# Two tiles of x begin 8 and 16 bytes behind a multiple of 256 bytes

## The chip, the cores and the metric

The kernel runs on one core of a Trainium2 chip. The metric is the device time of one execution in microseconds (us), as the median of several runs. The core has a matrix engine (TensorE, PE in the profile; its weight loads are listed apart as PEld), a vector engine (DVE), a scalar engine (ACT), a general engine (POOL) and an engine that only issues transfers (SP). Each works through its own queue in order.

## The reference

Attention over queries that are averaged in pairs, and a feed-forward block behind it:

```python
q_pool = q.reshape(B, H, S // 2, 2, D).mean(axis=3)      # B=8 H=8 S=1152 D=64
scores = scale * np.matmul(q_pool, k.transpose(0, 1, 3, 2))
attn = np.exp(scores - np.max(scores, axis=-1, keepdims=True))
attn = attn / (np.sum(attn, axis=-1, keepdims=True) + 1e-09)
x = np.matmul(attn, v)                   # then to 4608 tokens x 512
h = x @ w_in                             # 512 -> 2048
out = (h - np.tanh(h)) @ w_out           # 2048 -> 512
```

Everything is float32.

## The kernel before

**Attention.** Heads are handled in 32 pairs, one head on each half of the 128 partitions. Float32 precision is reached by splitting a value into a high part that TensorE takes in one pass (type F32R, tiles kq_h) and the rest (kq_l), and adding the products high x high, high x low and low x high. Each pair's 576 queries are done in two halves of 288 columns. The unnormalised result of a pair goes to a scratch tensor in memory, x_dram, and the sums of the exponentials to s_dram; their reciprocals come back through r_dram.

**Feed-forward.** The 4608 tokens are done in nine chunks of 512, and the 2048 inner columns in 16 steps of 128, so there are 144 steps. A step has two products. `hidden` makes 12 matmuls of 512 columns into ps_h: the stationary operand is a block of w_in (high or low), the moving operand a block x[:, c] of x_h or x_l, c = 0 to 3; eight of the twelve read x_h and four x_l. `shrink` computes h - tanh(h) on ACT, DVE and POOL, and splits it into g_hi and g_lo. `second` makes 12 matmuls of 512 columns into ps_o, with g as the stationary and w_out as the moving operand. Steps 0 to 2 are placed among the last three attention pairs; from about 796 us on only feed-forward steps are left. The last step of all does its `hidden` in two halves of 256 columns.

**x.** An object of class X holds one chunk's tiles. `fetch` brings 512 tokens of x_dram into the tile x_l in one transfer. `fetch_r` spreads the reciprocals over the partitions of x_r. For each c, `times` multiplies x_l by x_r into x_r, `high` copies that to x_h in the type F32R (ACT), and `low` writes the difference to x_l. For the first chunk these steps lie beside attention, with `times` and `low` on DVE; for the other eight they lie beside the steps of the chunk before, with `times` and `low` on POOL at steps 7 to 14, and the transfer issued at step 4 (for the second chunk, ahead of the loop). Chunks alternate between two pools of tiles, xp[0] and xp[1], each with one x_h and one x_l.

**Order.** The engines' queues are written by hand: the wrapper InOrder keeps the order of the program on each engine, which is why nearly all instructions carry its line, L37. The planner has no say in it. In front of the feed-forward the lengths of the tiles (x, the reciprocals, weights, g) are multiples of 256 bytes a partition, and they follow each other in memory in the order in which their pools are made; x of the first pool is the first of them.

**A start that is off, elsewhere.** The raw weights, 64 bits wide, are loaded twice from the same source: into w_raw at its start, and right behind it into w_off one 16-bit element in (`self.off[:, 1:4 * WN + 1]`).

Of the kernel before, what the change touches and what calls it, by code (L numbers as in the profile page):

```python
# [8 lines left out]
F32R = mybir.dt.float32r  # L9
# [37 lines left out]
def attention_ffn_kernel(  # L47
# [16 lines left out]
    P = 128  # L64
    B, NP, _, _, SQ = q.shape
# [26 lines left out]
    xp = [ctx.enter_context(tc.tile_pool(name="xp0", bufs=1))]  # L92
# [17 lines left out]
    class X:  # L110


        def __init__(self, ci):
            self.t0, self.n = chunks[ci]
            self.h = xp[ci % 2].tile([P, NP, 512], F32R, name="x_h")
            self.l = xp[ci % 2].tile([P, NP, 512], F32R, name="x_l")
            self.r = {}

        def fetch(self):
# [109 lines left out]
    with ExitStack() as actx:  # L229
# [27 lines left out]
        def psum():  # L257
            return ring.tile([P, 2, 512], F32, name="ps")
# [298 lines left out]
        for pi in range(n_pair):  # L557
# [7 lines left out]
            n = pi + EARLY - n_pair  # L565
            if n == 0:
                c = Chunk(0)
# [5 lines left out]
            for place in range(NS):  # L573
# [3 lines left out]
                if kt == 0:  # L577
                    o = psum()
# [28 lines left out]
    for ci in range(len(chunks)):  # L607
        if ci:
            c = Chunk(ci)
# [4 lines left out]
        for f in range(NF):  # L614
            n = ci * NF + f
# [76 lines left out]
```

## Time and profile before

| | us |
|---|---|
| median of 3 runs | 1580.07 |
| lowest and highest run | 1576.46 and 1581.28 |
| the profiled execution | 1580.02 |
| its span, from the first to the last instruction | 1578.3 |
| PE busy in the span | 1556.5 |
| DVE, POOL, ACT busy | 1185.8, 1155.3, 978.3 |

The granted clock of TensorE over the span was 0.999. In the profile's rows a group is named by line, engine, operation and tiles, written out<-in, with the shape as partitions x elements and a count; then come busy us, mean ns of one, and idle us ahead of it. In the timeline a row has start, length, and how many instructions were merged in it. Matmuls overlap in the records, so that their pace is read from their starts. DMA rows give packets, MB, and the share of 16 engines that the packets took.

### The profile page before, as it was taken

How to read it: one execution, taken by the hardware profiler on the slowest of the kernel's cores; microseconds unless marked ns; L12 is line 12 of the kernel's file. 1: busy time of each engine (PE TensorE's matmuls, PEld its weight loads, DVE VectorE, ACT ScalarE, POOL GpSimd, SP SyncE). 2: the span in 40 equal slices, each digit the busy share in tenths (PEclk: the TensorE clock that was granted, in tenths of full speed). 3: DMA queues.
4: the chain of work that ended last, by engine and by line, in shares of the span. 5: the costliest groups of instructions: out<-in, count | busy, mean ns of one | idle time of the engine just before them, and what ended most of it. 6: DMA issues, size and time to landing. Idle time of an engine off the chain costs nothing.

```text
span 1578.3 us, 30802 instructions
## 1 busy us (share of the span) xinstructions
PE 1556.5 (99%) x12012; PEld 1224.1 (78%) x12012; DVE 1185.8 (75%) x1558; ACT 978.3 (62%) x1617; POOL 1155.3 (73%) x813
## 2 busy tenths in 40 slices
PE   7999999999999999999999999999999999999998
PEld 5777777777777777676778888888888888888886
DVE  6588787888888887765457777777777777777776
ACT  5667667667667667675645655565555555565654
POOL 6788888898888897785857576666767575766664
PEclk9999999999999999999999999999999999999999
DMA  5757767768677769573171201010010101020000
GB/s 169 207 177 218 222 185 220 218 211 252 186 237 210 218 201 267 143 231 91 63 285 70 68 15 67 14 61 14 13 61 14 67 14 67 14 67 14 28 1 27
DMA packets 88676, 193.59 MB, mean 123 GB/s; under 512 B 12882, under 2 KB 39890, under 8 KB 86482
## 3 DMA queue, kind: packets, MB, share of 16 engines
q1 hardware_dynamic: 79746, 155.35, 27.4%
q0 software_dynamic: 8784, 36.28, 12.7%
q8 instruction: 94, 1.54, 0.4%
q14 instruction: 52, 0.43, 0.1%
HBM read 126.12 MB, written 38.04 MB: 104 GB/s over the span
## 4 chain that ended last, share of the span: by engine, by line
PE 91%; DMA 3%; ACT 2%; DVE 2%; issue 1%; SPq 0%; POOLq 0%; POOL 0%; ACTq 0%; DVEq 0%
PE ps L37 43%; PE ps_o L37 24%; PE ps_h L37 24%; ACT p L37 2%; DMA s_dram<-s_s 2%; DVE mx L37 1%; DMA m_row<-m_dram 0%; DMA x_r<-r_dram 0%; DMA m_dram<-tr 0%; DVE w_hl L37 0%; SPq L37 0%; DVE w_t L37 0%; DMA q<-in_q_dram 0%; DVE ps_w L37 0%; DVE x_r L37 0%
## 5 line engine op out<-in xcount | busy, mean ns | idle before, releaser
L37 DVE TENSOR_REDUCE mx<-ps 128x2 f32<-128x768 f32 x448 | 400.1, 924 | 145.2 <-PE ps L37 145.0
L37 POOL TENSOR_SCALAR g_m<-g_u 128x512 uint8<-128x512 f32 (+1 forms) x145 | 247.2, 1705 | 184.6 <-ACT g_u L37 170.3
L37 POOL TENSOR_TENSOR sum<-p,p 128x576 f32<-128x576 f32 x192 | 294.4, 1533 | 117.9 <-ACT p L37 117.9
L37 ACT ACTIVATE p<-ps 128x576 f32<-128x576 f32 x576 | 347.3, 653 | 48.0 <-PE ps L37 27.6
L37 POOL TENSOR_TENSOR sum<-sum,p 128x576 f32<-128x576 f32 x192 | 291.7, 1519 | 15.0
L37 PE MATMUL ps<-p,v 128*64 128x288 f32 x2304 | 286.4, 407 | 3.5 <-DVE mx L37 0.4
L37 PE MATMUL ps<-kq_h 64*128 64x288 f32 (+1 forms) x1920 | 273.4, 338 | 8.4 <-ACT kq_h L37 6.4
L37 PEld LDWEIGHTS ps<-p,v 128*64 128x64 f32 x2304 | 162.5, 137 | 119.6 <-ACT p L37 10.2
L37 POOL TENSOR_TENSOR g_lo<-g_s,g_hi 128x512 fp32r<-128x512 f32 (+1 forms) x145 | 186.9, 1289 | 87.4 <-ACT g_hi L37 87.4
L37 PE MATMUL ps_o<-w,g_hi 128*128 128x512 f32 x792 | 244.0, 389 | 1.0 <-ACT g_hi L37 1.0
L37 ACT ACTIVATE g_u<-ps_h 128x512 f32<-128x512 f32 (+1 forms) x142 | 84.0, 591 | 217.8 <-PE ps_h L37 216.3
L37 PEld LDWEIGHTS ps<-kq_h 64*128 64x128 f32 x1920 | 179.1, 186 | 49.6 <-issue 13.9
L37 DVE SCALAR_TENSOR_TENSOR ps_w<-g_u,ps_h 128x512 f32<-128x512 f32 (+1 forms) x142 | 98.4, 693 | 153.2 <-ACT g_t L37 153.2
L37 PE MATMUL ps_h<-x_h,w 128*128 128x512 f32 (+1 forms) x800 | 212.0, 387 | 0.1
L37 ACT ACTIVATE g_s<-g_u,pc 128x512 f32<-128x512 f32 x290 | 193.4, 715 | 11.4 <-POOL g_lo L37 0.2
L37 PE MATMUL ps<-m_row,sel 64*128 64x288 f32 x1152 | 171.4, 293 | 2.8 <-DMA m_row<-m_dram 2.2
L37 PEld LDWEIGHTS ps_o<-w,g_hi 128*128 128x128 f32 x792 | 148.5, 188 | 32.1 <-ACT g_hi L37 1.4
L37 PEld LDWEIGHTS ps_h<-x_h,w 128*128 128x128 f32 x800 | 149.3, 188 | 31.1 <-DVE g_t L37 0.5
L37 PE MATMUL ps<-kq_l,kq_h 64*128 64x288 f32 x1152 | 171.7, 293 | 0.0
L37 PE MATMUL ps<-kq_h,kq_l 64*128 64x288 f32 x1152 | 171.6, 293 | 0.0
L37 PE MATMUL ps_o<-w,g_lo 128*128 128x512 f32 x396 | 154.4, 390 | 0.1
L37 DVE COPY_PREDICATED g_s<-g_m,g_t 128x512 f32<-128x512 uint8 (+1 forms) x145 | 110.5, 762 | 17.0 <-POOL g_m L37 2.1
(114 smaller groups left out, 2379.7 us busy)
## 6 DMA issues: line engine op xcount, KB each, us to landing
kq_l<-raw POOLq DMA_DIRECT2D x31, 864.0 KB, 8.0
v<-in_v_dram SPq DMA_DIRECT2D x32, 576.0 KB
raw<-in_k_dram SPq DMA_DIRECT2D x31, 576.0 KB
x_dram<-o_s SPq DMA_DIRECT2D x32, 288.0 KB
x_l<-x_dram SPq DMA_DIRECT2D x9, 1024.0 KB
out_dram<-o_f SPq DMA_DIRECT2D x36, 256.0 KB
raw<-in_q_dram SPq DMA_DIRECT2D x30, 288.0 KB
raw<-in_q_dram POOLq DMA_DIRECT2D x30, 288.0 KB, 10.0
```

The costliest lines, as they stand in the source:

```text
L37: i = f(*args, **kwargs)
```

## The change

The tiles x_h and x_l are made 64 elements longer (2112 float32 values a partition instead of 2048). The data takes 2048 of them: in x_h from element 2 on (8 bytes), in x_l from element 4 on (16 bytes). All uses go through self.h and self.l, and so through the shifted view. No instruction is added, removed or moved.

```diff
         def __init__(self, ci):
             self.t0, self.n = chunks[ci]
-            self.h = xp[ci % 2].tile([P, NP, 512], F32R, name="x_h")
-            self.l = xp[ci % 2].tile([P, NP, 512], F32R, name="x_l")
+
+            self.h, self.l = (xp[ci % 2].tile([P, NP * 512 + 64], F32R, name=n)[:, o:o + NP * 512].rearrange(
+                "p (c n) -> p c n", c=NP) for n, o in (("x_h", 2), ("x_l", 4)))
             self.r = {}
```

## The prediction

> **What bounds the kernel now.** I read the page's busy shares first, then the stretches of the span, then the timeline of TensorE inside one stretch, and last the tiles that the change touches.
>
> ```profile
> span 1578.3 us, 30802 instructions
> PE 1556.5 (99%) x12012; PEld 1224.1 (78%) x12012; DVE 1185.8 (75%) x1558; ACT 978.3 (62%) x1617; POOL 1155.3 (73%) x813
> PE 91%; DMA 3%; ACT 2%; DVE 2%; issue 1%; SPq 0%; POOLq 0%; POOL 0%; ACTq 0%; DVEq 0%
> ```
>
> TensorE is busy 99% of the span and carries 91% of the chain that ended last. DVE, ACT and POOL stay at 75% or below. A busy PE could still hide waits, so the stretches (columns: length, then busy us and instructions of PE, weight loads, DVE, ACT, POOL, then clock):
>
> ```profile
> 100.00:900.00 800.00, 793.22 (x8110) 601.30 (x8108) 609.40 (x724) 522.76 (x839) 641.41 (x447) 1.00 0.65 193
> 1200.00:1300.00 100.00, 100.00 (x442) 82.78 (x442) 75.35 (x109) 59.51 (x103) 66.80 (x47) 1.00 0.09 32
> 796.20:1570.00 773.80, 406.67 (x1704) 318.29 (x1704) 194.54 (x283) 165.54 (x284) 1.00 0.14 48
> ```
>
> The third row counts only instructions on ps_h, the product of x with w_in. So 1704 of the matmuls that read x lie in the feed-forward stage, where TensorE is busy 100.00 of 100 us; the last stretch, after 796 us, is one unbroken stream of matmuls, at granted clock 1.00. Anything that x's address does to a matmul there goes straight into the time, and anything that it does to another engine is hidden until that engine runs out of slack.
>
> The timeline shows what one such matmul costs (start, length, and a group of so many):
>
> ```profile
> 1474.54 1.07 PE L37 MATMUL ps_h<-x_l,w 128*128 128x512 f32 x4
> 1475.44 1.07 PE L37 MATMUL ps_h<-x_h,w 128*128 128x512 f32 x4
> 1476.35 0.61 PE L37 MATMUL ps_o<-w,g_hi 128*128 128x512 f32 x2
> 1476.80 0.39 PE L37 MATMUL ps_o<-w,g_lo 128*128 128x512 f32 x1
> ...
> 1479.98 1.07 PE L37 MATMUL ps_h<-x_l,w_raw 128*128 128x512 f32 x4
> ...
> 1559.43 0.64 PE L37 MATMUL ps_h<-x_l,w 128*128 128x256 f32 x4
> 1559.91 1.12 PE L37 MATMUL ps_h<-x_h,w 128*128 128x256 f32 x8
> ```
>
> Starts, not lengths, give the price, since the lengths overlap. Four of 512 columns take 1475.44 - 1474.54 = 0.90 us, and the four behind them 0.91: 226 to 227 ns each. Four of 256 columns take 1559.91 - 1559.43 = 0.48 us, 120 ns each. So 256 columns cost about 106.6 ns (0.416 ns a column), and about 13.4 ns of each matmul do not depend on its columns. x_h, x_l and the second product (1476.80 - 1476.35 = 0.45 for two) all run at the same pace today.
>
> **The change, part by part.** It adds no instruction, no transfer and no wait, and moves none on any queue. x_h and x_l become 64 elements longer (2112 instead of 2048 a partition); the data starts 2 elements (8 bytes) in for x_h and 4 elements (16 bytes) in for x_l. Each tile is 256 bytes longer, so what lies behind in memory shifts by 512 bytes and keeps its place against 256. What can change is the time of the instructions that touch x:
>
> ```profile
> L37 PE MATMUL ps_h<-x_l,w x400: 283/389/389, 810.9 to 1561.2; 128*128 128x512 f32 x131, 128*128 128x256 f32 x3
> L37 POOL TENSOR_TENSOR x_r<-x_l,x_r x32: 1284/1294/1307, 828.1 to 1470.0; 128x512 f32<-128x512 f32 x32
> L37 POOL TENSOR_TENSOR x_l<-x_r,x_h x32: 1290/1299/1302, 834.3 to 1476.2; 128x512 fp32r<-128x512 f32 x32
> L37 SPq DMA_DIRECT2D x_l<-x_dram x9: 385/386/577, 598.3 to 1407.1; - x9
> L37 DVE TENSOR_TENSOR x_r<-x_l,x_r x4: 650/974/1887, 614.5 to 683.2; 128x512 f32<-128x512 f32 x4
> L37 DVE TENSOR_TENSOR x_l<-x_r,x_h x4: 627/904/1126, 618.3 to 684.5; 128x512 fp32r<-128x512 f32 x4
> L37 ACT ACTIVATE x_h<-x_r x36: 631/634/637, 615.8 to 1471.4; 128x512 fp32r<-128x512 f32 x36
> ```
>
> *The matmuls.* 1704 in the feed-forward stage and 36 (three steps of 12) before it make 1740; two thirds read x_h (1160), one third x_l (580). The trace has no matmul whose moving operand starts 8 or 16 bytes off. The nearest is the query half: both halves are 288 columns of one tile, the first at its start, the second 1152 bytes in, which is 128 behind a multiple of 256.
>
> ```profile
> 405.25 0.29 PE L37 MATMUL ps<-kq_h 64*128 64x288 f32 x2
> 405.38 0.29 PE L37 MATMUL ps<-kq_l,kq_h 64*128 64x288 f32 x2
> 405.51 0.30 PE L37 MATMUL ps<-kq_h,kq_l 64*128 64x288 f32 x2
> ...
> 410.36 0.29 PE L37 MATMUL ps<-kq_h 64*128 64x288 f32 x2
> 410.49 0.29 PE L37 MATMUL ps<-kq_l,kq_h 64*128 64x288 f32 x2
> 410.62 0.30 PE L37 MATMUL ps<-kq_h,kq_l 64*128 64x288 f32 x2
> ```
>
> The pairs follow each other by 0.13 us in the first half (405.25, 405.38, 405.51) and in the second (410.36, 410.49, 410.62). So 128 bytes off costs nothing, and I take 0. Bounds: from below, the 13.4 ns that do not depend on columns, gone altogether: -1740 x 13.4 = -23 us. From above, the slowest pace at which this program streams columns. The plain f32 product of p and v has, per pair of 288 columns,
>
> ```profile
> L37 PE MATMUL ps<-p,v 128*64 128x288 f32 x2304 | 286.4, 407 | 3.5 <-DVE mx L37 0.4
> ```
>
> 286.4 us over 1152 pairs, 249 ns or 0.865 ns a column against 0.416. At that pace a matmul of x costs 0.449 x 512 = 230 ns more: 1160 x 230 = +267 us for x_h alone, +400 for both.
>
> The Trainium skill, page "SBUF — State Buffer", section "Specifications (TRN2)", says that the memory is read in lines of 16 bytes, that two hits on a line are needed for full bandwidth, and that each step to a new line is paid for. By it x_l, 16 bytes off, keeps 128 lines a matmul, and x_h, 8 bytes off, touches 129, the two end lines with two hits each; if the extra line costs the time of four columns (an estimate: 4 x 0.416 = 1.7 ns), the sum would be 1160 x 1.7 = +1.9 us higher. No run here shows it, and it would be too small to tell from no change.
>
> *The transfer into x_l*, nine times 1 MB. A row for a start that is off exists: the raw weights are loaded twice from the same source, once into w_raw at its start and, issued directly behind it, into w_off 2 bytes in. Two windows, the first while the copy into w_raw runs, the second while the one into w_off does (queue: packets, MB, share of 16 engines):
>
> ```profile
> q1 hardware_dynamic: 253, 1.03, 71.6%
> q0 software_dynamic: 108, 0.21, 31.5%
> ...
> q1 hardware_dynamic: 570, 1.44, 101.4%
> ```
>
> 71.6% of 16 engines over 3.6 us is 41.2 engine-us for 1.03 MB, 40.0 a MB; 101.4% is 58.4 for 1.44 MB, 40.6 a MB. A start 2 bytes off costs under 2%, so I take 0. From above, the accumulating queue over the whole span:
>
> ```profile
> q1 hardware_dynamic: 79746, 155.35, 27.4%
> q0 software_dynamic: 8784, 36.28, 12.7%
> ```
>
> 12.7% of 16 x 1578.3 us for 36.28 MB is 88.4 engine-us a MB, 27.4% for 155.35 MB is 44.5. A write at the slower rate would add 44 engine-us a MB, 2.9 us on 16 engines, to a fetch of 1.05 MB. Eight of the nine are issued three steps or more, of 5.44 us (1479.98 - 1474.54), before they are first read, and are covered. Only the first (598.3 us) lies in a busy queue ahead of x_r, for which the chain of waits has DVE waiting:
>
> ```profile
> 609.37 5.05 DMA x_r<-r_dram
> ```
>
> There the whole 2.9 us could show.
>
> The page "DMA: Bandwidth & Descriptors", section "How a descriptor splits into AXI transactions", of the Trainium skill, says that a descriptor that does not start at a multiple of 256 bytes needs one transaction more. For pieces of 2048 bytes that makes nine instead of eight; the first fetch would be an eighth longer, and the sum +0.3 us. The two windows above show no such eighth, so the row decides.
>
> *POOL, ACT, DVE.* The last x_l of a chunk and the gaps around it:
>
> ```profile
> 1470.04 1.29 POOL L37 TENSOR_TENSOR x_r<-x_l,x_r 128x512 f32<-128x512 f32 x1
> 1472.64 1.49 POOL L37 TENSOR_SCALAR g_m<-g_u 128x512 uint8<-128x512 f32 x1 [1.31 <-ACT g_u L37]
> 1474.94 1.30 POOL L37 TENSOR_TENSOR g_lo<-g_s,g_hi 128x512 fp32r<-128x512 f32 x1 [0.81 <-ACT g_hi L37]
> 1476.19 1.30 POOL L37 TENSOR_TENSOR x_l<-x_r,x_h 128x512 fp32r<-128x512 f32 x1
> 1477.45 1.50 POOL L37 TENSOR_SCALAR g_m<-g_u 128x512 uint8<-128x512 f32 x1
> ```
>
> That x_l is done at 1477.49; its first reader, the fourth matmul of the group at 1479.98, starts at 1480.66: 3.2 us of cover. If both POOL steps doubled, they would add 2.6 us in two steps, against 1.31 + 0.81 us of gaps in view and those 3.2; still hidden. ACT's 634 ns has as much room. The eight DVE instructions on the first chunk run beside attention; doubled, they add 4 x 0.97 + 4 x 0.90 = 7.5 us at most. I take 0 for all three; they run at 1.2 to 2.5 ns a column, three times slower than TensorE reads, so a start off a boundary presses them less.
>
> *Sum*: 0 + 0 + 0 against the profiled execution of 1580.02 us (span 1578.3 and 1.7 around it), which stands at the median of 1580.07. Forecast 1580 us, own range 1575 to 1585, since the runs before already spread over 1576.46 to 1581.28 and about 0.3% (4.7 us) is what can be told from no change.
>
> **Rivals.**
> 1. *Slower: each matmul on an off-boundary row pays its start again.* The place is TensorE from 796 us on, the price the 13.4 ns above. For x_h alone 1160 x 13.4 = 15.5 us, 1595.5 in all; for both 23.3 us, 1603. It decides (0.3%) from 2.7 ns a matmul. For it: the stream has no gap to absorb a nanosecond, and no row is off by less than 128 bytes. Against it: that row shows nothing. 0.20.
> 2. *Much slower: every four columns of x_h need two reads and the stream falls to the f32 pace*, 1580 + 267 = 1847. For it: these matmuls take a column each 0.416 ns, twice the pace of the f32 ones, so a feed at its limit has no reserve. Against it: the same query rows. 0.09.
> 3. *Faster: part of the 13.4 ns comes from x starting at the same boundary as the weights loaded beside it.* Half of it gone is 1740 x 6.7 = 11.7 us, 1568. Against it: the second product, with other tiles, pays the same. 0.07.
>
> **How the numbers follow.** No change has 0.64. Rivals 1 and 2 are slower (0.29), 3 faster (0.07). No change and rival 1 hold 0.84, so the range is 1575 to 1604.
>
> **What would show it.** Right: ps_h groups still start 0.90 to 0.91 us apart by fours, x_l's POOL steps stay near 1294 and 1299 ns, ACT's near 634. Rival 1: the ps_h groups rise to 0.96 us while ps_o stays. If x_h rises and x_l does not, 8 bytes matter and 16 don't. Rival 2: ps_h<-x_h near 1.8 us by fours. Were the time to move with ps_h's pace unchanged, the cause would lie before 796 us, and my cover for the first chunk's fetch and DVE steps would be what failed.

## The result, and the profile after

The changed kernel takes 1598.55 us (median of 4 runs, 1592.60 to 1599.37) against 1579.03 us before (median of 4): a ratio of 1.0124, 95% interval 1.011 to 1.0138. It is slower by 19.5 us. The forecast was no change; the time lies inside the stated range, close to the 1595.5 us of rival 1.

The page of the changed kernel, its busy shares and its chain:

```profile
span 1597.2 us, 30802 instructions
PE 1573.5 (99%) x12012; PEld 1229.9 (77%) x12012; DVE 1185.3 (74%) x1558; ACT 978.1 (61%) x1617; POOL 1144.7 (72%) x813
PE 91%; DMA 3%; ACT 2%; DVE 2%; issue 1%; SPq 0%; POOLq 0%; POOL 0%; ACTq 0%; DVEq 0%
```

The shares look as before. What moved is the busy time of PE, up by 17.0 us with the same 12012 instructions; DVE, ACT and POOL are not busier. A stretch of 100 us in the feed-forward, still of the changed kernel (the columns are those of the prediction's stretches):

```profile
1200.00:1300.00 100.00, 100.00 (x434) 81.70 (x433) 74.60 (x109) 57.52 (x100) 64.51 (x47) 1.00 0.11 35
```

TensorE is busy 100.00 of 100 us as before and at clock 1.00, but does 434 matmuls in place of 442. The timeline over one step of the changed kernel shows which are late (start, length, count):

```profile
1474.27 1.10 PE L37 MATMUL ps_h<-x_h,w 128*128 128x512 f32 x4
1475.21 1.09 PE L37 MATMUL ps_h<-x_l,w 128*128 128x512 f32 x4
1476.13 1.11 PE L37 MATMUL ps_h<-x_h,w 128*128 128x512 f32 x4
1477.07 0.63 PE L37 MATMUL ps_o<-w,g_hi 128*128 128x512 f32 x2
1477.54 0.39 PE L37 MATMUL ps_o<-w,g_lo 128*128 128x512 f32 x1
1477.77 0.62 PE L37 MATMUL ps_o<-w,g_hi 128*128 128x512 f32 x2
...
1479.14 0.61 PE L37 MATMUL ps_o<-w,g_hi 128*128 128x512 f32 x2
1479.59 0.39 PE L37 MATMUL ps_o<-w,g_lo 128*128 128x512 f32 x1
1479.82 1.09 PE L37 MATMUL ps_h<-x_h,w 128*128 128x512 f32 x4
```

Groups of four that read x start 0.94, 0.92 and 0.94 us after one another, where it was 0.90 to 0.91. The second product, which does not read x, is late too at first: two of its matmuls take 1477.54 - 1477.07 = 0.47 us, at its end 1479.59 - 1479.14 = 0.45 as before. One step takes 1479.82 - 1474.27 = 5.55 us. Taken over all complete steps of the trace it is 5546.7 ns against 5440.0 ns before, the same to a nanosecond in every step: a loss of 106.7 ns, as much as 256 columns at the 0.416 ns a column that the prediction read off. About 80 ns of it lie in the starts behind the twelve matmuls of the first product, 27 in those of the second. 139 such steps make 14.8 us.

The rest of the span's 18.9 us, 4.1, lies before the feed-forward stands alone: its first step starts at 803.13 us in place of 799.07. The stretch ahead of it, before (first fence) and after (second):

```profile
700.00:795.00 95.00, 92.48 (x953) 68.22 (x955) 47.35 (x64) 55.70 (x94) 71.28 (x52) 0.98 0.34 97
```

```profile
700.00:795.00 95.00, 90.65 (x928) 68.37 (x926) 45.52 (x64) 56.46 (x94) 68.61 (x51) 0.96 0.35 101
```

The granted clock was 0.98 and 0.96 there. It varies between executions of one kernel: with the data back at 0 (e1_pad below) it was 0.96 in the profile as well, and with x_h alone off (e2_h8) 1.00. The one run of the changed kernel whose clock was 1.000 over the span took 1592.60 us, 13 to 16 us more than the runs of the kernel before at that clock (1576.16 to 1579.12); the 14.8 us of the steps agree with that. So these 4 us are not put down to the change here; with 4 runs of it, it stays open whether it makes the dip more frequent.

The other users of x, in the changed kernel:

```profile
L37 POOL TENSOR_TENSOR x_r<-x_l,x_r x32: 1281/1290/1308, 832.7 to 1487.2; 128x512 f32<-128x512 f32 x32
L37 POOL TENSOR_TENSOR x_l<-x_r,x_h x32: 1088/1092/1107, 838.8 to 1493.3; 128x512 fp32r<-128x512 f32 x32
L37 ACT ACTIVATE x_h<-x_r x36: 630/634/636, 616.8 to 1488.5; 128x512 fp32r<-128x512 f32 x36
```

None is slower. POOL's subtraction became faster, 1299 to 1092 ns; it is hidden, so nothing came of it.

### The profile page after: what moved, and what is told of

Its sections match the earlier page's. It is cut to its first block, busy times and chain, and to the rows that moved or that the text cites. A ratio compares the mean times of both kernels' runs of the same rounds, so it can differ in the third digit from the quotient of the medians.

```text
span 1597.2 us, 30802 instructions
## 1 busy us (share of the span) xinstructions
PE 1573.5 (99%) x12012; PEld 1229.9 (77%) x12012; DVE 1185.3 (74%) x1558; ACT 978.1 (61%) x1617; POOL 1144.7 (72%) x813
## 4 chain that ended last, share of the span: by engine, by line
PE 91%; DMA 3%; ACT 2%; DVE 2%; issue 1%; SPq 0%; POOLq 0%; POOL 0%; ACTq 0%; DVEq 0%
PE ps L37 42%; PE ps_h L37 25%; PE ps_o L37 24%; ACT p L37 2%; DMA s_dram<-s_s 2%; DVE mx L37 1%; DMA m_row<-m_dram 0%; DMA x_r<-r_dram 0%; DMA m_dram<-tr 0%; DVE w_hl L37 0%; SPq L37 0%; DVE w_t L37 0%; DMA q<-in_q_dram 0%; DVE ps_w L37 0%; DVE x_r L37 0%
## 5 line engine op out<-in xcount | busy, mean ns | idle before, releaser
L37 POOL TENSOR_SCALAR g_m<-g_u 128x512 uint8<-128x512 f32 (+1 forms) x145 | 242.4, 1672 | 198.4 <-ACT g_u L37 183.2
L37 PE MATMUL ps_h<-x_h,w 128*128 128x512 f32 (+1 forms) x800 | 218.2, 395 | 0.0
```

The costliest lines, as they stand in the source:

```text
L37: i = f(*args, **kwargs)
```

## The experiments

In the tables below "excess" is the time of a feed-forward step over 5440 ns, from the starts of the first product's groups, as a mean over steps 9 to 13 of a chunk, unless other steps are named. The granted clock was 1.00 there in all traces, and in the chunks named a step's time repeats within a few ns.

**e1_pad, e2_h8, e3_l16: which part of the change.** The three kernels differ from the changed one in the two starts:

```diff
-                "p (c n) -> p c n", c=NP) for n, o in (("x_h", 2), ("x_l", 4)))
+                "p (c n) -> p c n", c=NP) for n, o in (("x_h", 0), ("x_l", 0)))   # e1_pad
+                "p (c n) -> p c n", c=NP) for n, o in (("x_h", 2), ("x_l", 0)))   # e2_h8
+                "p (c n) -> p c n", c=NP) for n, o in (("x_h", 0), ("x_l", 4)))   # e3_l16
```

> The tiles are 256 bytes longer as in the changed kernel, but the data starts at 0 in both. Theory A (TensorE pays for where a row of x_h lies within 16 bytes): as before, about 1579 us and 5440 ns a feed-forward step. Theory B (any start off a multiple of 32 or more costs): the same here. Theory C (the longer tiles or the shift of everything behind them by 512 bytes is the cause): about 1597 us, 5547 ns a step.

> x_h starts 8 bytes in, x_l at 0. Theory A (only the 8 bytes cost): all of the loss, about 1597 us, a step of 5530 to 5547 ns, with the matmuls of x_l back at 226.7 ns. Theory B (each row off costs alike): two thirds of it, about 1592 us, a step of about 5510 ns.

> x_h starts at 0, x_l 16 bytes in. Theory A: as before, 1579 us, 5440 ns a step. Theory B: one third of the loss, about 1585 us, a step of about 5475 ns.

Ratios to the kernel before: e1_pad 1.0009 (0.9994 to 1.0024), e2_h8 1.0109 (1.0077 to 1.0141), e3_l16 1.0040 (1.0020 to 1.0061). Steps: 5440.0, 5546.7 and 5486.7 ns. The longer tiles and the shift behind them cost nothing, which ends theory C. The timelines of e2_h8 and then e3_l16:

```profile
1300.07 1.10 PE L37 MATMUL ps_h<-x_h,w 128*128 128x512 f32 x4
1301.01 1.09 PE L37 MATMUL ps_h<-x_l,w 128*128 128x512 f32 x4
1301.93 1.10 PE L37 MATMUL ps_h<-x_h,w 128*128 128x512 f32 x4
...
1305.62 1.10 PE L37 MATMUL ps_h<-x_h,w 128*128 128x512 f32 x4
```

```profile
1299.97 1.07 PE L37 MATMUL ps_h<-x_h,w 128*128 128x512 f32 x4
1300.88 1.09 PE L37 MATMUL ps_h<-x_l,w 128*128 128x512 f32 x4
1301.80 1.09 PE L37 MATMUL ps_h<-x_h,w 128*128 128x512 f32 x4
1302.73 0.63 PE L37 MATMUL ps_o<-w,g_hi 128*128 128x512 f32 x2
...
1305.46 1.07 PE L37 MATMUL ps_h<-x_h,w_raw 128*128 128x512 f32 x4
```

With x_h off, x_l's group is late too (0.92 us) though it starts at 0. With x_l off, the x_h group ahead of it takes 0.91 and x_l 0.92; the x_h group behind it, in place itself, takes 0.93 by its starts. So lateness is carried on to matmuls that are not off themselves. And 106.7 + 46.7 is not 106.7: the parts don't add. Theory A fell, since 16 bytes cost; theory B got e3's ratio about right (1.004) but not the step of e2, which had the whole 106.7 ns in place of two thirds.

**e4_quiet: are other engines part of it?** In the feed-forward, shrink is left out:

```diff
-            if n >= EARLY:
-                shrink(s, steps[n - 1])
+            if n == EARLY:
+                g_high(steps[n - 1])
+                g_low(steps[n - 1])
+            if n >= EARLY:
+                s.g_h, s.g_l = steps[n - 1].g_h, steps[n - 1].g_l
```

> Offsets of 8 and 16 as in the changed kernel; from the fourth step on, the work of shrink on ACT, DVE and POOL is left out, and all second products use the g of the third step, so that TensorE is nearly alone in the feed-forward. Theory A1 (a row at 8 bytes costs TensorE by itself, for one line more): the matmuls of x_h stay at 230 to 236 ns, those of x_l and the second product at 226.7. Theory A2 (a row at 8 bytes only makes TensorE collide with what the other engines read and write): all matmuls go back to 226.7 ns, 5440 ns a step.

```profile
1200.00:1300.00 100.00, 100.00 (x435) 81.66 (x434) 0.00 (x0) 4.92 (x8) 9.46 (x8) 1.00 0.10 32
```

With DVE at 0.00, ACT at 4.92 and POOL at 9.46 us in 100, the step is 5546.7 ns again, and each of its 24 intervals is the one of the changed kernel. The work of the other engines is not needed for the loss. Transfers go on in this run (share 0.10). This ended A2, and A1 as well in its part that x_l and the second product would go back.

**s1_both and s2_h: the size of the offset.** Since each chunk makes its own x, one run can try nine starts:

```diff
+            oh, ol = ((0, 0), (1, 1), (2, 2), (3, 3), (4, 4), (6, 6), (8, 8), (16, 16), (32, 32))[ci]   # s1_both, elements
```

> Each chunk of tokens has its own start, the same for x_h and x_l: chunks 0 to 8 at 0, 4, 8, 12, 16, 24, 32, 64 and 128 bytes. Step times by chunk. Theory L (lines of 16 bytes): 4, 8, 12 and 24 bytes cost, 16, 32, 64 and 128 cost nothing; the 46.7 ns of x_l at 16 bytes already speak against it. Theory G (a coarser grain, 32 or 64 bytes): all below the grain cost about 107 to 160 ns a step, the multiples of the grain 0. Theory W (the distance between the rows of x and the weights loaded beside them): the cost changes with every distance, 32 and 64 bytes included, 128 perhaps 0.

> x_l at 0; x_h at 0, 4, 12, 16, 20, 32, 48, 64 and 128 bytes in chunks 0 to 8. Theory L: 4, 12 and 20 cost, 16, 32, 48 and 64 nothing. Theory G: 16 bytes cost twice what x_l at 16 costs (8 matmuls in place of 4): about 93 ns a step; the multiples of the grain 0. Theory W: as in the run where both start alike, by distance.

| start, bytes | 0 | 4 | 8 | 12 | 16 | 20 | 24 | 32 | 48 | 64 | 128 |
|---|---|---|---|---|---|---|---|---|---|---|---|
| s1_both, excess ns | 0 | 160 | 107 | 67 | 87 | | 100 | 120 | | 93 | 87 |
| s2_h (x_l at 0), excess ns | 0 | 120 | | 67 | 73 | 127 | | 93 | 107 | 87 | 67 |

Two rows of s1_both, chunk 1 (4 bytes), a step apart:

```profile
920.25 1.12 PE L37 MATMUL ps_h<-x_h,w 128*128 128x512 f32 x4
...
925.85 1.12 PE L37 MATMUL ps_h<-x_h,w 128*128 128x512 f32 x4
```

5.60 us. No start between 4 and 128 bytes is free and the cost has no order in it, which ends theories L and G as accounts of the moving operand: neither a line of 16 bytes nor a grain of 32 or 64 gives 87 ns at 128. What the prediction cited from the Trainium skill, page "SBUF — State Buffer", section "Specifications (TRN2)", that lines of 16 bytes count, would have let 16, 32, 64 and 128 bytes go free; the measurement decides against it as the whole account.

**s3_weights, s4_rows, b2_order: weights off, single rows off, another order.** From s3_weights on, the kernels have two output buffers in place of three (b2_order and b1_all32 apart), and step 3 of a chunk is longer in them; steps 9 to 13 are free of that. Code left out of a line is marked with three dots.

```diff
+                load_w(... wt.tile([P, 1088], F32R, name=f"w{which}_{f}")[:, 2:1026], f, which)   # s3: w_in of steps 5 to 15
+    self.h = Rows([t[:, c * 576 + o:c * 576 + o + 512] for c, o in enumerate(offs)])      # s4: one start for each block of x_h
+    mm = {2: hh + hw + ll, 3: ll + hh + hw, 4: mix, ...}.get(s.chunk.t0 // 512, hh + ll + hw)  # b2
```

> The blocks of w_in of steps 5 to 15 start 8 bytes in, those of steps 0 to 4 at 0; x_h and x_l alike at 0, 8, 16, 4, 32, 64, 0, 24 and 12 bytes in chunks 0 to 8. Theory W: in the chunk where x starts 8 bytes in, steps 5 to 15 cost nothing (5440 ns) and steps 0 to 4 about 107 ns more; in the chunk where x starts at 0, steps 5 to 15 cost about 107 ns more. Theories L and G, if only the moving operand counts: steps 5 to 15 cost the same as 0 to 4 in every chunk, and nothing at 0.

> The four blocks of x_h have their own starts, each 2304 bytes behind the one before; x_l at 0. Chunks 0 to 8: none off; block 0 by 8 bytes; block 3 by 8; blocks 0 and 1 by 8; all by 8; block 0 by 16; block 3 by 16; all by 16; blocks 0 and 2 by 8. If each matmul on a row that is off pays for itself (32 cycles of TensorE, 13.3 ns): one block 26.7 ns a step (it is read twice), two 53.3, four 106.7, and the lateness ends within a few matmuls. If it is the change from one start to another that costs: one block costs as much as two neighbours, and all four less than two separate ones.

> x_h starts 8 bytes in, x_l at 0; the order of the twelve matmuls of the first product differs by chunk (h for x_h, l for x_l): chunks 0 and 1 hhhh llll hhhh, chunk 2 eight h then four l, chunk 3 four l then eight h, chunk 4 hlh four times, chunk 5 hh ll hhhh ll hh, chunk 6 ll, eight h, ll, chunk 7 llll, h, h, six h, chunk 8 lll, eight h, l. If each off matmul pays: 5547 ns in all chunks. If each entry into a run of off rows pays: about half of the 107 ns with one run (chunks 2, 3, 6, 7, 8), 107 with two (chunk 1), 160 or more with four and five (chunk 4).

s3_weights: with x at 0 and only the w_in blocks 8 bytes in, the excess is 53 ns (chunks 0 and 6); with both 8 bytes in, 100. A stationary operand 8 bytes off costs as well, so it is not the moving one alone; theory W's forecast of nothing for both alike fell in that form.

s4_rows: one block of four off by 8 bytes 53 ns, be it block 0 or 3; two neighbours 73; blocks 0 and 2 67; all four 107. By 16 bytes: one block 87, all four 73, so one row off can cost more than four. b2_order: two runs of rows off 107, one run of eight 80 in chunks 2, 3, 6 and 8 and 87 in chunk 7, three runs 93 (chunk 5), and five runs 107 (chunk 4, the order x_h, x_l, x_h four times). Neither "each matmul pays 13.3 ns" nor "each entry pays" gives these numbers.

**b1_all32: everything shifted alike.** The kernel before with one constant tile longer, so that all that follows starts 32 bytes behind a multiple of 256:

```diff
-    pc = const.tile([P, 32], F32, name="pc")
+    pc = const.tile([P, 40], F32, name="pc")
```

> The kernel before, with one small constant tile ahead of all others 32 bytes longer, so that x, the weights, g and all the rest start 32 bytes behind a multiple of 256; their distances from one another stay. Theory D (distances between the streams that TensorE reads decide): no change, 1577 us, 5440 ns a step. Theory N (each start's own place against a multiple of 256 decides): at least the 120 ns a step that x alone costs at 32 bytes, so 1594 us or more.

Ratio 0.9998 (0.9984 to 1.0012), steps of 5440.0 ns; x alone at 32 bytes had cost 120. The timeline:

```profile
1302.50 1.07 PE L37 MATMUL ps_h<-x_h,w_raw 128*128 128x512 f32 x4
1303.41 1.07 PE L37 MATMUL ps_h<-x_l,w_raw 128*128 128x512 f32 x4
1304.31 1.07 PE L37 MATMUL ps_h<-x_h,w_raw 128*128 128x512 f32 x4
...
1307.94 1.07 PE L37 MATMUL ps_h<-x_h,w_off 128*128 128x512 f32 x4
```

A multiple of 256 is not needed: with the distances between the tiles kept, a start 32 bytes behind it costs nothing, as theory D had it.

**b3_g, b4_wo: the operands of the second product.** g is its stationary operand, w_out its moving one.

```diff
+        s.g_h = gp.tile([P, 576], F32R, name="g_hi", bufs=LAG + 1)[:, oh:oh + 512]                # b3
+                load_w(wt.tile([P, 1088], F32R, name=f"w{which}_{f}")[:, 2:1026] if which ..., f, which)     # b4
```

> Starts of x (both tiles) and of g (both tiles, the stationary operand of the second product), in bytes, chunks 0 to 8: 0 and 0; 256 and 0; 0 and 8; 0 and 32; 0 and 128; 8 and 8; 32 and 32; 128 and 128; 0 and 8 for g_hi alone. The weight tiles of the first product and the moving operand of the second stay at 0. x at 256: 5440 ns if 256 is the period. Theory D and theory N both: g off alone costs, about the 53 ns that w_in's blocks cost at 8 bytes. Theory D: x and g off alike costs less than the sum of both.

> The blocks of w_out of steps 5 to 15, the moving operand of the second product, start 8 bytes in; x (both tiles) at 0, 0, 8, 32, 64, 128, 16, 4 and 0 bytes in chunks 0 to 8. Moving operands off cost alike in either product: steps 5 to 15 of chunk 1 about 107 ns more than 5440. Theory D: in chunk 2, where every moving operand starts at 8, less than in chunks 3 to 5, where they differ. Theory N: in chunk 2 about the sum, 200 ns.

b3_g: x at 256 bytes costs 0 ns, so for x 256 counts as 0. g off alone: 53 ns at 8 bytes, 87 at 32, 113 at 128; 53 with g_hi alone. x and g off alike: 147, 160 and 153, less than the sums of 160, 207 and 200, as theory D forecast, but far from free. b4_wo: w_out off alone 100 ns, near the 107 of x. With all moving operands at 8 bytes (chunk 2) it is 160. Theory D expected less there than in chunks 3 to 5, which have 142, 93 and 127, and theory N about 200; both missed.

**c1 to c4, d1, d2: one distance in all 24 matmuls.** Here all four operands of steps 5 to 15 can be placed: w_in and w_out by kernel, x and g by chunk.

```diff
+    w_all = [wt.tile([P, 11 * 1024 + 64], F32R, name=f"w_all{i}") for i in range(2)]
+                a = (f - 5) * 1024 + (2, 2)[which]       # c1_all8: both at 2 elements; others alike
+                load_w(w_all[which][:, a:a + 1024], f, which)
```

> All blocks of w_in and w_out of steps 5 to 15 start 8 bytes in; x (both tiles) and g (both) start, chunks 0 to 8, at 0 and 0; 8 and 8; 0 and 0; 8 and 0; 0 and 8; 32 and 32; 8 and 8; 0 and 0; 8 and 8. All else stays at multiples of 256. If the four streams that TensorE reads count only against one another: chunks 1, 6 and 8 at 5440 ns from step 7 on, though every one of the four starts 8 bytes off. If the other engines' tiles, or the multiple of 256 itself, count: 5540 ns or more there.

> Blocks of w_in of steps 5 to 15 at 8 bytes, those of w_out at 0; x and g, chunks 0 to 8: 0 and 0; 0 and 8; 0 and 0; 8 and 8; 8 and 0; 0 and 8; 32 and 32; 32 and 8; 0 and 8. Chunks 1, 5 and 8: every stationary operand 8 bytes in, every moving one at 0. If only the size of the distance counts: the 160 ns that all moving operands at 8 with all stationary at 0 cost. If its sign counts (the one that leads): another cost, more or less.

> Blocks of w_out of steps 5 to 15 at 32 bytes, w_in at 0; x and g, chunks 0 to 8: 0 and 0; 32 and 0; 0 and 0; 32 and 32; 128 and 0; 32 and 0; 8 and 0; 64 and 0; 32 and 32. Chunks 1 and 5: every moving operand 32 bytes ahead of its stationary one. If any distance off 256 costs each matmul alike: 160 ns a step, as at 8 bytes. If the cost goes with the bytes left to the next multiple of something: another number, which the run at 128 then orders.

> As the run before with 128 bytes: w_out at 128; x and g, chunks 0 to 8: 0 and 0; 128 and 0; 0 and 0; 128 and 128; 32 and 0; 128 and 0; 8 and 0; 64 and 0; 128 and 128. Chunks 1 and 5: every moving operand 128 bytes from its stationary one. If each matmul pays alike at any distance: 160 ns a step. If what x alone costs at 128 bytes (86.7 ns) came from the two changes between the products, and not from the distance: 0 to 50 ns here.

> All blocks of w_in and w_out of steps 5 to 15 start 32 bytes in; x and g, chunks 0 to 8: 0 and 0; 32 and 32; 0 and 0; 32 and 0; 0 and 32; 32 and 32; 64 and 64; 8 and 8; 32 and 32. All else at multiples of 256. If the distance between the operands that TensorE reads decides, and beside it where a row starts within 32 bytes: chunks 1, 5 and 8 at 5440 ns from step 7 on, as when every tile was shifted by 32. If shifting every tile was free because the tiles that TensorE does not read moved too: about 5590 ns, as with all four at 8 bytes.

> The same with 16 bytes: w_in and w_out of steps 5 to 15 at 16; x and g, chunks 0 to 8: 0 and 0; 16 and 16; 0 and 0; 16 and 0; 0 and 16; 16 and 16; 32 and 32; 8 and 8; 16 and 16. If the place within 16 bytes is what costs when all four are at 8: chunks 1, 5 and 8 at 5440 ns from step 7 on. If the place within 32 or more: above 5440, up to the 153 ns of all four at 8.

| moving operands, bytes | stationary, bytes | run | excess ns |
|---|---|---|---|
| 8 | 0 | b4_wo, chunk 2 | 160 |
| 16 | 0 | d2_all16, steps 0 and 1 of chunks 1 and 3 | 120 |
| 32 | 0 | c3_mov32, chunks 1 and 5 | 160 |
| 128 | 0 | c4_mov128, chunks 1 and 5 | 160 |
| 0 | 8 | c2_stat8, chunks 1, 5 and 8 | 96 |
| 0 | 16 | d2_all16, steps 5 and 6 of chunk 4 | 0 |
| 8 | 8 | c1_all8, chunks 1, 6 and 8 | 153 |
| 16 | 16 | d2_all16, chunks 1, 5 and 8 | 80 |
| 32 | 32 | d1_all32, chunks 1, 5 and 8 | 0 |

The step of c1_all8 with all four at 8 bytes, and that of d1_all32 with all four at 32:

```profile
918.01 1.09 PE L37 MATMUL ps_h<-x_h,w_all 128*128 128x512 f32 x4
...
923.60 1.09 PE L37 MATMUL ps_h<-x_h,w_all 128*128 128x512 f32 x4
```

```profile
924.49 1.07 PE L37 MATMUL ps_h<-x_h,w_all 128*128 128x512 f32 x4
...
929.93 1.07 PE L37 MATMUL ps_h<-x_h,w_all 128*128 128x512 f32 x4
```

5.59 us against 5.44. In chunk 0 of d1_all32 the same weights at 32 bytes meet x and g at 0:

```profile
835.31 1.10 PE L37 MATMUL ps_h<-x_h,w_all 128*128 128x512 f32 x4
...
840.91 1.10 PE L37 MATMUL ps_h<-x_h,w_all 128*128 128x512 f32 x4
```

5.60 us. So d1 answers what c1 had left open: the tiles that TensorE does not read can stay where they are, and moving and stationary operands off alike are free at 32 bytes, but not at 16 (80 ns) or 8 (153 ns); the first of c1's alternatives, 5440 ns at 8 bytes, did not come. A distance in all 24 matmuls costs 160 ns, 6.7 ns a matmul, at 8, 32 and 128 bytes alike when the moving operand is the one that is off, and 120 at 16; c4's second alternative, 0 to 50 ns, did not come either. When the stationary one is off by 8 bytes it is 96, so it also counts which of the two is off.

One run also shows a distance that is free. In steps 5 and 6 of chunk 4 of d2_all16, x starts at 0 and w_in at 16, and the second product, two steps behind, still has w_out at 0 with g at 16:

```profile
1166.97 1.07 PE L37 MATMUL ps_h<-x_h,w_all 128*128 128x512 f32 x4
1167.88 1.07 PE L37 MATMUL ps_h<-x_l,w_all 128*128 128x512 f32 x4
1168.78 1.07 PE L37 MATMUL ps_h<-x_h,w_all 128*128 128x512 f32 x4
1169.69 0.62 PE L37 MATMUL ps_o<-raw,g_hi 128*128 128x512 f32 x2
...
1172.41 1.07 PE L37 MATMUL ps_h<-x_h,w_all 128*128 128x512 f32 x4
```

That is 5.44 us. So every stationary operand can start 16 bytes from its moving one at no cost, while 8 bytes cost 96 ns, and w_in alone 32 bytes in (steps 5 and 6 of chunk 0 of d1_all32) costs 87. Distance alone is therefore not the rule.

The free steps are of two kinds. In one, the moving and the stationary operand start at the same place against 256 bytes, and that place is a multiple of 32; places 0, 32 and (for x) 256 were tried, all four at 64 or 128 were not. In the other, the moving operand is at 0 and the stationary one at 16. The same place is thus enough where it was 0 or 32, but it is not needed in every case. No placement was faster than 5440 ns, so none beats the kernel before.

## Why the prediction was right or wrong

- *What bounds the kernel*: right. The feed-forward is TensorE's stream at 100.00 of 100 us, and what the starts did to a matmul went into the time, 14.8 us for 139 steps.
- *The matmuls, taken at 0*: this is the step that failed. The term measures 106.7 ns a step, about 15 us. The row that I took as nearest, the two query halves 128 bytes apart, was near in address but not in kind: those matmuls read 64 rows, two side by side on the array, at 288 columns, and show no cost at 128 bytes, while the 128-row matmuls of the feed-forward pay 87 ns a step for x at 128 bytes. I took absence in one shape for absence in the other; no run shows which of the differences between the two matters. The bounds, -23 and +267 us, held.
- *The extra line of 16 bytes, +1.9 us*: the place within a line is not the cause by itself; 16 to 128 bytes cost as well.
- *The transfer, at 0*: nothing of it shows. The loss of 14.8 us stands in the pace of TensorE in every step. But the two windows could not settle the extra transaction as the prediction has it: their pieces are of 4096 bytes, twice those of x, so one more transaction would be less than an eighth there.
- *POOL, ACT, DVE, at 0*: right for the time; ACT takes 634 ns as before, POOL's two steps 1290 and 1092.
- *Rival 1*: right in its place and, by chance, in its price. Its 13.4 ns for each of 1160 matmuls of x_h make 15.5 us, and 106.7 ns are 8 x 13.3. But the mechanism is not a start paid again by each row that is off: one block off costs 53 ns and four 107, x_l at 16 bytes adds nothing to x_h at 8, and five matmuls of the second product carry part of it. Its against, that the query rows show nothing, weighed too much at a chance of 0.20.
- *Rival 2*: not seen. The groups of x_h start 0.94 us after one another, not 1.8.
- *Rival 3* said that x's start against the weights' could matter, as a gain. The distance does matter, but no value was better than 0: the 13.4 ns of a matmul stayed in every placement tried.
- *The sign that was to tell 8 bytes from 16*, whose group rises, cannot do so: in e2_h8 the group of x_l rises to 0.92 us at a start of 0, since lateness is carried on.

What is not settled: why a start costs what it does, why a stationary operand 16 bytes off is free, and why the numbers of mixed placements have no order. They are the same in every step and need no work of another engine, so the cause is looked for in TensorE; no run shows what happens there.

## What to carry to other kernels

Where TensorE's stream is the bound, give the moving and the stationary operand of a matmul the same place against 256 bytes, 0 or 32, which were free here; the simplest way is to make every tile in front a multiple of 256 bytes long and to start each operand at the tile's start. In the placements that cost anything it is worth 0.9 to 3.4% of a step of 24 matmuls of 128 rows and 512 columns (47 to 187 ns of 5440). When a price is taken from the nearest row, ask that it be near in the shape of the instruction as well as in the quantity that changes, and read starts of matmuls, not busy shares: these were 99% before and after.

## What the runs showed of the hardware that I had not expected

- TensorE's pace depends on where its operands start against each other: x 128 bytes off costs as much as 16 bytes off (87 ns a step), shifting all tiles by 32 bytes costs nothing (a ratio of 0.9998), and stationary operands 16 bytes off alone cost nothing either (5440 ns).
- Lateness is passed on: matmuls whose operands are all in place start 2 to 9 ns behind their pace when they follow others that are not (five of them in the changed kernel).
- POOL's subtraction x_l = x_r - x_h takes 1092 ns in place of 1299 with x_h 8 bytes in. In s1_both its mean is 1095 to 1099 ns at 4, 8 and 24 bytes and 1292 to 1300 at 12, 16, 32, 64 and 128; there the multiplication by x_r, which reads x_l, falls to 1088 to 1103 at 8, 12 and 24.
